# One visit for the experts' down product, a 128-row turn, and a split first weight load in a fused attention and expert kernel

## The chip, the cores and the metric

The kernel runs on one core of a Trainium2 chip. The core has TensorE (matrix products out of SBUF into PSUM), VectorE, ScalarE and GpSimd (element work), and SyncE, whose queue issues most of the transfers between HBM and SBUF; 16 DMA engines move the data. The time is the device's, in microseconds, for one whole execution, and what is compared is the median of several runs.

## The reference, cut to what matters

Two things are computed from one input x of 2048 rows and 1024 columns and mixed row by row with a gate g: a linear attention with 32 heads whose features are softmaxes, and one expert, a gated feed-forward net that sees a single row of x (the one with the largest r) and adds its result to that row alone.

```python
def reference(A_x, A_wqkv, A_w_phi, A_wo, B_x, B_w_r, B_w_gate, B_w_up, B_w_down, gate_w):
    ...
        pq = jnp.einsum("bhsd,hdf->bhsf", q, w_phi)
        pk = jnp.einsum("bhsd,hdf->bhsf", k, w_phi)
        phi_q = jnp.concatenate([_softmax(pq, axis=-1), _softmax(-pq, axis=-1)], axis=-1)
        phi_k = jnp.concatenate([_softmax(pk, axis=-1), _softmax(-pk, axis=-1)], axis=-1)
        kv = jnp.einsum("bhsf,bhsd->bhfd", phi_k, v)
        z  = jnp.einsum("bhsf->bhf", phi_k)
        num = jnp.einsum("bhqf,bhfd->bhqd", phi_q, kv)
        den = jnp.einsum("bhqf,bhf->bhq", phi_q, z)[..., None] + 1e-6
        o = num / den
    ...
        g = _silu(x_sel @ w_gate)
        u = x_sel @ w_up
        y = (g * u) @ w_down
    ...
    x = A_x
    g = _sigmoid((x * gate_w).sum(-1, keepdims=True))
    a = _A_ref(x, A_wqkv, A_w_phi, A_wo)
    b = _B_ref(x, B_w_r, B_w_gate, B_w_up, B_w_down)
    return g * a + (1 - g) * b
```

The expert's hidden width is 3584, so its three weight matrices are 7.3 MB each; all of them are read for the sake of one row.

## The kernel before

The 2048 rows are 16 tiles of 128 (`NT`); x stands transposed in `xT`, with the 1024 columns as 8 blocks of 128 (`KB`). The feature matrix `w_phi` is folded into the key and query weights (`kfold`, `qfold`), so that a feature unit is one product of x with a folded weight: eight 512-column matmuls for a tile and half the heads, 32 units for the keys and 32 for the queries (`NU` = 32).

The program has four stretches in time.

First the value product. `v_first` (from line 611 in the rows) takes row tiles 0 and 1, transposes them on TensorE (line 299), and then goes block by block through the value weights `wv_sb`, which SyncE's queue loads in eight transfers of 256 KB, one for each block (line 282). The columns are cut at `VC` = 0, 256, 640, 1026 into three parts c; block 0 is taken for both tiles with parts 0 and 1 ahead of part 2, blocks 1 to 6 in rounds of six matmuls. Behind the weight loads the same queue issues transposing loads of the further x tiles (line 305), four small loads of `w_phi` and transposing loads of the key and query weights (line 312). Tiles 2 to 15 follow with `k_v` (line 594); the folds of the key weights (line 322) stand after tiles 4, 6, 8 and 9.

Then a loop over steps i. Steps 0 to 31 make the key units (`feats`, line 640) and, five steps later (`LAG`), their sums with the values (`k_kv`, line 671). Steps 32 to 63 make the query units; each unit's features are turned by a transposing DMA on SyncE's queue (line 688, `phT`), and some steps later `q_num` (line 705) multiplies them with the key-value sums, which ScalarE copies out of PSUM at step 36 (`kv_finish`, line 680). The output product (`q_wo`, line 744) follows when a counter of TensorE time, `pe`, says so.

The expert is strewn between these steps. At steps 9, 16 and 23 `ffn_gu` (line 530) makes the gate and up sums: four column strips of 32 run side by side in the array, so the matmuls are marked 128\*32. Their rows are gathered in `gT`, an FP32 tile of 128 partitions that was set to zero at the start and of which 64 rows are filled. At step 29 `ffn_turn` (line 494) turns `gT` into 56 columns of `ffn_ps` by a product with `identf`, with rows 0 to 63 of both. At step 38 (`DN` = 38) `ffn_down(0, 4)` starts the down product, and at step 41 (`DN2` = 3) `ffn_down(4, 7)` ends it: chunk c is four blocks of 128 rows of the down weights, each block is two matmuls of 512 columns (line 548), also on four column strips, so 32 and 24 matmuls. The seven loads of 1 MB each (line 490) are in the code of `ffn_down(0, 4)`; their buffers are those that the gate and up weights leave. `moe_cols`, behind the second visit, copies the sums out of PSUM (line 558), and four small DMAs on SyncE's queue pick the rows (line 560). `moe_sum`, `moe_scale`, `moe_out` and `moe_spread` are placed 4, 6, 7 and 10 steps after `DN + DN2`.

Order: the code above is a list of operations with their dependencies. A planner lays each engine's instructions out from it, earliest possible first, except for what `pin` keeps in place. So a load may stand in a queue long before the step in whose code it is, while TensorE, which always has work ready, runs nearly in the order of the steps.

```python
    DN, DN2 = NU + 6,3
        if i == DN:
            ffn_down(0, 4)
        if i == DN + DN2:
            ffn_down(4, 7)
            moe_cols()
```

Of the kernel before, what the change touches and what calls it, by code (L numbers as in the profile page):

```python
# [20 lines left out]
D = 1024  # L21
# [8 lines left out]
NU = NT * 2  # L30
# [4 lines left out]
VC = [0, 256, 640, 1026]  # L35
# [135 lines left out]
def kernel(  # L171
# [4 lines left out]
    nc = tc.nc  # L176
    x2 = A_x.rearrange("b s d -> (b s) d")
    out2 = out.rearrange("b s d -> (b s) d")
    w_v = A_wqkv.rearrange("(kb p) n -> p kb n", p=P)
# [22 lines left out]
    pin = tc.keep_in_program_order  # L202
# [28 lines left out]
    identf = const.tile([P, 56], F32, name="identf")  # L231
    nc.vector.tensor_copy(out=identf[:], in_=ident[:, 0:56])
    nc.vector.tensor_tensor(out=identf[:, 48:56], in0=identf[:, 48:56], in1=ident[:, 56:64], op=ALU.add)
    gT = const.tile([P, P], F32, name="gT")
# [15 lines left out]
    ffn_ps = small_ps[:, 0:64]  # L250
# [19 lines left out]
    def xload(t, eng):  # L270
        xt_ = shv[1][:, 2 + t, :]
        pin(eng.dma_start(out=xt_, in_=x2[t * P:(t + 1) * P, :]))
        xtiles[t] = xt_

    wv_sb = w16.tile([P, KB, VW], BF, name="wv_sb", tag="w16")
# [3 lines left out]
    for kb in range(KB):  # L279
        if kb == 0:  # L280
            xload(1, nc.sync)
        pin(nc.sync.dma_start(out=wv_sb[:, kb, 0:D], in_=w_v[:, kb, 2 * D:3 * D]))

    def rows_in():
        rows_ps = m2_ps[:, 0:2 * KB]
# [202 lines left out]
    def wd_load(c, where):  # L488
        w = wbuf(where).rearrange("p (b n) -> p b n", b=4)
        nc.sync.dma_start(out=w, in_=wd_v[:, c * 4:(c + 1) * 4, :])  # L490
        return w

    def ffn_turn():
        nc.tensor.matmul(ffn_ps[:, 0:56], lhsT=gT[0:64, :], rhs=identf[0:64, :], start=True, stop=True)

    def ffn_mid():
        sg = const.tile([P, NFB], F32, name="sg")
# [43 lines left out]
    def ffn_down(c0, c1):  # L541
        if c0 == 0:
            moe["wd"] = [wd_load(c, p) for c, p in enumerate("AAADDWV")]
        ws = moe["wd"]
        for blk in range(4 * c0, 4 * c1):
            for n in range(2):
                g = (blk % 2) * 2 + n
                nc.tensor.matmul(small_ps[32 * g:32 * g + 32, :], lhsT=hh32[:, blk, :],  # L548
                                 rhs=ws[blk // 4][:, blk % 4, n * 512:(n + 1) * 512], start=(blk < 2),
                                 stop=(blk >= NFB - 2), tile_position=(0, 32 * g), skip_group_check=True)  # L550

    def moe_cols():
        ym = ring.tile([P, D * 2], F32, name="ym", tag="wch")
        ys = ym[:, 0:512]
        y4 = ym[0:KB, 512:768].rearrange("p (s c) -> p s c", s=2)
        ybc = ym[:, 1280:1792].bitcast(BF)
        moe["ybc"] = ybc
        nc.scalar.copy(out=ys, in_=small_ps[:])
        for g in range(4):
            nc.sync.dma_start(out=y4[4 * (g % 2):4 * (g % 2) + 4, g // 2, :], in_=ys[32 * g:32 * g + 1, :])  # L560
        moe["y4"] = y4
# [238 lines left out]
    QT0, QT1 = (4, 7)  # L800
    GU = (9, 16, 23)
    TU = 29
    DN, DN2 = NU + 6,3
    TF, TNUM, TWO, TKV = 1.73, 0.27, 1.73, 0.27
    L_NUM0, N_1, L_NUM1, L_NUM, L_WO0, L_WO, MOST = 11.0, 6, 15.0, 10.5, 8, 6, 2
    pe = 0.0
# [3 lines left out]
    i = 0  # L810
    while i < 2 * NU or n_next < NU or wos:
# [8 lines left out]
        if i == 28:  # L820
            moe["wo"] = w16.tile([P, KB, D], BF, name="wo_sb", tag="w16")
            nc.gpsimd.tensor_copy(out=moe["wo"][0:1, 0, 0:1], in_=kst[i - 1][0:1, 0, 0, 0:1])
            nc.sync.dma_start(out=moe["wo"][:], in_=A_wo.rearrange("(kb p) n -> p kb n", p=P))
        if i == DN:
            ffn_down(0, 4)
        if i == DN + DN2:
            ffn_down(4, 7)
            moe_cols()
            qp["oo"] = wob.tile([P, 16, 512], BF, name="oo", tag="wo")
            qp["n_oo"] = 0  # L830
            qp["late"] = []
# [27 lines left out]
        if i == TU:  # L859
            ffn_turn()  # L860
            ffn_mid()
# [93 lines left out]
```

## Time and profile before

| what | us |
|---|---|
| median of 3 runs (265.38 to 265.94) | 265.49 |
| the profiled execution, its own time | 264.34 |
| its span, first to last instruction | 262.7 |
| TensorE busy (98% of the span) | 258.3 |
| VectorE, ScalarE, GpSimd busy | 176.2, 128.1, 126.3 |

Rows of the trace come from the one profiled execution. In a timeline each row is a run of like instructions: its start, the time from its first start to its last end, engine, line, tiles, shape and count. A matmul is pipelined: the printed time of one (0.38 us for 512 columns) reaches past the start of the next, so the cost of a matmul on TensorE is read from start to start. The mark 128\*128, 128\*32 or 64\*128 is the part of the array that a matmul takes, rows by columns. PEld rows are the weight loads that go ahead of the matmuls. An idle time in brackets names what ended it; "issue" means nothing that the profile shows.

### The profile page before, as it was taken

The page shows a single profiled execution, that of the slowest core. Times are in us where ns is not written, and L with a number is a line of the kernel's source. Part 1 is how long each engine was busy: PE and PEld are TensorE (multiplying, and loading weights), DVE is VectorE, ACT ScalarE, POOL GpSimd, SP SyncE. Part 2 cuts the span into 40 slices and gives each one's busy share as a digit, 9 for nine tenths or more (in the row PEclk, how much of TensorE's full clock was granted, in tenths as well). Part 3 has the DMA queues.
Part 4 walks back from the last instruction along what each step waited for, and adds up shares of the span by engine and source line. Part 5 has one row for each costly group of instructions (what it writes and reads, how often), then busy time and mean ns, then how long its engine had stood idle before and what let it go on. Part 6 is the DMA issues. An engine that isn't in the chain of part 4 may idle for free.

```text
span 262.7 us, 5700 instructions
## 1 busy us (share of the span) xinstructions
PE 258.3 (98%) x2190; PEld 137.3 (52%) x2190; DVE 176.2 (67%) x309; ACT 128.1 (49%) x264; POOL 126.3 (48%) x86
## 2 busy tenths in 40 slices
PE   8999999999999999999999999999999999999995
PEld 4666666665444554545455455455444544454443
DVE  3111103015599676997888799799898797888873
ACT  3135536356766454654457677447362553535220
POOL 7000000000175998679989887655535545454101
PEclk9999999999999999999999999999999999999999
DMA  6999999949999959989968997997989697879642
GB/s 220 267 138 188 169 177 186 187 94 364 406 349 162 227 145 415 395 300 368 376 201 317 218 153 200 223 203 136 261 179 232 139 225 164 211 144 192 165 126 82
DMA packets 110971, 58.47 MB, mean 223 GB/s; under 512 B 93580, under 2 KB 98780, under 8 KB 110940
## 3 DMA queue, kind: packets, MB, share of 16 engines
q1 hardware_dynamic: 108252, 53.73, 84.3%
q10 hardware_dynamic: 2656, 4.33, 6.2%
q8 instruction: 18, 0.29, 0.5%
q14 instruction: 13, 0.11, 0.1%
q0 software_dynamic: 32, 0.00, 0.0%
HBM read 31.27 MB, written 4.20 MB: 135 GB/s over the span
## 4 chain that ended last, share of the span: by engine, by line
PE 95%; DVE 2%; ACT 1%; issue 0%; ACTq 0%; DVEq 0%
PE pq L640 21%; PE po L744 21%; PE pk L640 20%; PE pv L594 18%; PE kvps L671 3%; PE num L705 3%; PE facc L530 2%; PE pv L611 1%; PE vbank L611 1%; PE small_ps L548 1%; PE small_ps L206 1%; PE vbank L322 1%; DVE wfT L343 1%; DVE xT L301 1%; PE vbank L338 0%
## 5 line engine op out<-in xcount | busy, mean ns | idle before, releaser
L658 POOL TENSOR_TENSOR phi<-e,rq 128x1024 bf16<-128x1024 bf16 x63 | 119.6, 1912 | 65.2 <-DVE rq L654 50.0
L650 DVE TENSOR_REDUCE ssum<-e 128x32 f32<-128x1024 bf16 x64 | 77.4, 1211 | 16.6 <-ACT e L646 16.5
L640 PEld LDWEIGHTS <-xT 128*128 128x128 bf16 x512 | 47.3, 97 | 52.7 <-issue 1.4
L640 PE MATMUL pq<-wqf,xT 128*128 128x512 bf16 x256 | 60.3, 379 | 0.0
L640 PE MATMUL pk<-wkf,xT 128*128 128x512 bf16 x256 | 59.9, 379 | 0.1
L744 PE MATMUL po<-wo_sb,oT 128*128 128x512 bf16 (+2 forms) x264 | 60.0, 372 | 0.0
L594 PE MATMUL pv<-wv_sb,xT 128*128 128x256 bf16 (+2 forms) x336 | 50.2, 307 | 0.0
L594 PEld LDWEIGHTS <-xT 128*128 128x128 bf16 x336 | 31.9, 97 | 16.1 <-issue 0.5
L645 ACT ACTIVATE e<-pq 128x512 bf16<-128x512 f32 x32 | 18.9, 592 | 36.1 <-PE pq L640 35.7
L602 ACT CAST v_all<-pv 128x384 bf16<-128x384 f32 (+1 forms) x45 | 20.1, 450 | 33.5 <-PE pv L594 25.1
L744 PEld LDWEIGHTS <-oT 128*128 128x128 bf16 x264 | 23.9, 98 | 23.3
L645 ACT ACTIVATE e<-pk 128x512 bf16<-128x512 f32 x32 | 19.2, 599 | 27.2 <-PE pk L640 21.8
L748 DVE SCALAR_TENSOR_TENSOR oo<-po,gate,xg 128x512 bf16<-128x512 f32 (+2 forms) x33 | 24.0, 727 | 4.4 <-PE po L744 4.3
L472 POOL COPY wch<-shv 1x1 bf16<-1x1 bf16 x3 | 0.4, 176 | 52.5 <-DMA shv<-in_A_wqkv_dram 52.5
L654 DVE RECIPROCAL rq<-ssum 128x32 f32<-128x32 f32 x64 | 21.8, 342 | 1.3
L326 DVE CAST wkf<-vbank 128x512 bf16<-128x512 f32 x8 | 5.2, 687 | 25.8 <-PE pW L322 25.8
L710 DVE TENSOR_TENSOR o_sb<-num,rden 128x512 bf16<-128x512 f32 x32 | 21.6, 674 | 0.8
L646 ACT ACTIVATE e<-pk 128x512 bf16<-128x512 f32 x32 | 19.0, 594 | 0.0
L646 ACT ACTIVATE e<-pq 128x512 bf16<-128x512 f32 x32 | 18.9, 590 | 0.0
L729 ACT ACTIVATE xg<-xin,omg 128x1024 f32<-128x1024 bf16 x16 | 18.4, 1148 | 0.4
L705 PEld LDWEIGHTS <-phT 128*128 128x128 bf16 x256 | 12.4, 98 | 7.8 <-issue 0.5
L343 DVE CAST wfT<-vbank 128x512 bf16<-128x512 f32 x8 | 5.2, 683 | 16.1 <-PE pW L338 16.1
(134 smaller groups left out, 155.2 us busy)
## 6 DMA issues: line engine op xcount, KB each, us to landing
wch<-in_B_w_down_dram SPq DMA_DIRECT2D x7, 1024.0 KB
wch<-in_B_w_up_dram SPq DMA_DIRECT2D x6, 1024.0 KB
wch<-in_B_w_gate_dram SPq DMA_DIRECT2D x4, 1024.0 KB
xin<-in_A_x_dram ACTq DMA_DIRECT2D x16, 256.0 KB
out_dram<-oo SPq DMA_DIRECT2D x31, 128.0 KB
wch<-in_B_w_gate_dram SPq DMA_DIRECT2D x4, 768.0 KB
wv_sb<-in_A_wqkv_dram SPq DMA_DIRECT2D x8, 256.0 KB
wo_sb<-in_A_wo_dram SPq DMA_DIRECT2D x1, 2048.0 KB
```

The lines of the kernel that those rows point to most:

```text
L594: nc.tensor.matmul(pv[:, 0:hi - lo], lhsT=xT[:, kb, t * P:(t + 1) * P], rhs=wv_sb[:, kb, lo:hi], start=(kb == 0), stop=(kb == KB - 1))
L602: copy(out=v_all[:, t, h0:h1, 0:DH], in_=pv[:, 0:(h1 - h0) * DH].rearrange("p (h d) -> p h d", d=DH))
L640: nc.tensor.matmul(pk[:].rearrange("p (c r) f -> p c r f", r=4) if is_q else pkf, lhsT=xT[:, kb, t * P:(t + 1) * P], rhs=q_heads(wf, kb, h ...
L645: nc.scalar.activation(out=e[:, :, 0, :], in_=pk[:], func=ACTF.Exp)
L646: nc.scalar.activation(out=e[:, :, 1, :], in_=pk[:], func=ACTF.Exp, scale=-1.0)
L650: nc.vector.tensor_reduce(out=ssum[:], in_=e2, axis=AX.X, op=ALU.add)
L654: nc.vector.reciprocal(out=rs, in_=ssum[:])
L658: eng.tensor_tensor(out=phi[:].rearrange("p h s f -> p (h s) f"), in0=e2, in1=_bc(rs, [P, HH * 2, DH]), op=ALU.mult)
L705: nc.tensor.matmul(num[:, pl * 66:pl * 66 + 66], lhsT=phT[:, pl, :], rhs=KV[hf][:, pl, :], start=True, stop=True)
L710: nc.vector.tensor_tensor(out=st["o"][:, hf * HH:(hf + 1) * HH, :].rearrange("p (r h) d -> p r h d", h=2), in0=nv[:, :, :, 0:DH], in1=rden ...
L744: nc.tensor.matmul(po[:, 0:w], lhsT=st["oT"][:, kb, :], rhs=moe["wo"][:, kb, sl], start=(kb == 0), stop=(kb == KB - 1))
L748: nc.vector.scalar_tensor_tensor(out=o_out[:, 0:w], in0=po[:, 0:w], scalar=gate[:, t:t + 1], in1=st["xg"][:, sl], op0=ALU.mult, op1=ALU.add)
```

## The change

Three edits. The down product becomes one visit of 56 matmuls at step 40, `ffn_down(0, 7)`, with its loads, its sums' copies and the steps that hang on `DN + DN2` one step earlier than before (the copy `hh32` stays at step 35). The turn of the gate and up sums uses all 128 rows of `gT` and `identf`, of which rows 64 and up are zero. The load of block 0 of the value weights is issued as two transfers, columns 0 to 255 and 256 to 1023.

```diff
     for kb in range(KB):
         if kb == 0:
             xload(1, nc.sync)
-        pin(nc.sync.dma_start(out=wv_sb[:, kb, 0:D], in_=w_v[:, kb, 2 * D:3 * D]))
+        for lo, hi in ((0, VC[1]), (VC[1], D)) if kb == 0 else ((0, D),):
+            pin(nc.sync.dma_start(out=wv_sb[:, kb, lo:hi], in_=w_v[:, kb, 2 * D + lo:2 * D + hi]))
...
     def ffn_turn():
-        nc.tensor.matmul(ffn_ps[:, 0:56], lhsT=gT[0:64, :], rhs=identf[0:64, :], start=True, stop=True)
+        nc.tensor.matmul(ffn_ps[:, 0:56], lhsT=gT[:], rhs=identf[:], start=True, stop=True)
...
-    DN, DN2 = NU + 6,3
+    DN, DN2 = NU + 6, 2
...
-        if i == DN:
-            ffn_down(0, 4)
         if i == DN + DN2:
-            ffn_down(4, 7)
+            ffn_down(0, 7)
             moe_cols()
```

## Rows read from the trace of the kernel before

**Rows 1.** The page's busy table: engine, busy us, share of the span, instructions.
```profile
PE 258.3 (98%) x2190; PEld 137.3 (52%) x2190; DVE 176.2 (67%) x309; ACT 128.1 (49%) x264; POOL 126.3 (48%) x86
```
**Rows 2.** TensorE's timeline, 135.9 to 138: start, length, engine, line, operation, tiles, count.
```profile
135.97 1.89 PE L640 MATMUL pq<-wqf,xT 128*128 128x512 bf16 x8
137.69 0.42 PE L671 MATMUL kvps<-v_all,phi 128*128 128x66 bf16 x8
```
**Rows 3.** TensorE's timeline at the first down visit, 147.3 to 148.9 and 143 to 160.
```profile
147.12 0.38 PE L640 MATMUL pq<-wqf,xT 128*128 128x512 bf16 x1
...
147.43 1.91 PE L548 MATMUL small_ps<-wch,hh 128*32 128x512 bf16 x32
149.28 1.90 PE L640 MATMUL pq<-wqf,xT 128*128 128x512 bf16 x8
```
**Rows 4.** TensorE's timeline at the second down visit, 143 to 160.
```profile
155.32 1.48 PE L548 MATMUL small_ps<-wch,hh 128*32 128x512 bf16 x24
156.74 1.90 PE L640 MATMUL pq<-wqf,xT 128*128 128x512 bf16 x8
```
**Rows 5.** Line 490, the loads of the down weights: duration min/median/max, first and last start.
```profile
L490 SPq DMA_DIRECT2D wch<-in_B_w_down_dram x7: 367/467/3902, 102.5 to 133.1; - x7
```
**Rows 6.** Timelines of SyncE's queue and of ScalarE ahead of the down product.
```profile
142.85 11.70 SPq L688 DMA_TRANSPOSE phT<-phi  x6
...
146.24 0.38 ACT L680 CAST KV<-kvps 64x264 bf16<-64x264 f32 x1
```
**Rows 7.** SyncE's queue in the first 24 us, and TensorE at 23 us.
```profile
1.78 3.75 SPq L282 DMA_DIRECT2D wv_sb<-in_A_wqkv_dram  x8
...
17.54 1.31 SPq L312 DMA_TRANSPOSE shv<-in_A_wqkv_dram  x1
...
23.12 0.19 PE L322 MATMUL vbank<-BDm,shv 32*128 32x32 bf16 x3
```
**Rows 8.** Timelines of TensorE and of its weight loads at the turn, 131.0 to 132.1.
```profile
131.07 0.38 PE L640 MATMUL pk<-wkf,xT 128*128 128x512 bf16 x1
131.38 0.42 PE L494 MATMUL small_ps<-identf,gT 64*128 64x56 f32 x2
131.74 0.43 PE L671 MATMUL kvps<-v_all,phi 128*128 128x66 bf16 x8
...
131.38 0.29 PEld L494 LDWEIGHTS small_ps<-identf,gT 64*128 64x128 f32 x2 [0.42 <-issue]
```
**Rows 9.** TensorE's timeline at a small full-array product, 108.2 to 109.2.
```profile
108.61 0.17 PE L421 MATMUL small_ps<-hlb,const-bfloat16-1.0 128*128 128x2 bf16 x1
108.64 0.41 PE L671 MATMUL kvps<-v_all,phi 128*128 128x66 bf16 x8
```
**Rows 10.** TensorE's timeline in the first value product, 5 to 12.7.
```profile
4.77 0.58 PE L299 MATMUL pT<-ident,shv 128*128 128x128 bf16 x6
5.18 0.47 PE L611 MATMUL vbank<-wv_sb,xT 128*128 128x256 bf16 x2
...
6.30 0.60 PE L611 MATMUL vbank<-wv_sb,xT 128*128 128x256 bf16 x3
6.75 0.60 PE L611 MATMUL pv<-wv_sb,xT 128*128 128x256 bf16 x3
7.30 0.60 PE L611 MATMUL vbank<-wv_sb,xT 128*128 128x256 bf16 x3
```
**Rows 11.** DMA packets of three stretches, in order 4.5:5.5, 5.5:9.25 and 10.5:11.75.
```profile
DMA packets 135, 0.25 MB, mean 246 GB/s; under 512 B 15, under 2 KB 15, under 8 KB 135
...
DMA packets 781, 1.43 MB, mean 381 GB/s; under 512 B 84, under 2 KB 84, under 8 KB 781
...
DMA packets 1394, 0.35 MB, mean 279 GB/s; under 512 B 1394, under 2 KB 1394, under 8 KB 1394
```
**Rows 12.** TensorE's timeline at a late start in the query steps, 210.8 to 211.7.
```profile
210.53 0.81 PE L640 MATMUL pq<-wqf,xT 128*128 128x512 bf16 x3
211.38 0.42 PE L705 MATMUL num<-KV,phT 128*128 128x66 bf16 x8
```

## The prediction

> **What bounds the kernel now.** I read the page's busy table first: TensorE works through 98% of the span [rows 1]. So a gain has to be time that TensorE loses between matmuls, and a loss has to be a new wait of TensorE; what VectorE, ScalarE, GpSimd and the queues save counts for nothing unless TensorE was waiting for it. Next I read TensorE's timeline, where one thing must be watched: matmuls overlap, so the duration printed is not their cost. The cost is the distance from one start to the next. In a plain stretch eight 512-column matmuls of the query projection start at 135.97 and the next group at 137.69 [rows 2]: 1.72 / 8 = 0.215 us each, and the eight 66-column matmuls behind them are as dense. Against this beat I looked for starts that come late, at the three places of the change. All three show one.
>
> **Part 1, the down product in one visit.** The last query matmul ahead of the first visit starts at 147.12 [rows 3]; at 0.215 us the next would start at 147.335, but the first down matmul starts at 147.43: 0.095 us lost on entry. The visit is 32 matmuls, four at a time on the four column strips, so eight groups; 149.28 - 147.43 = 1.85 us, less 8 x 0.215 = 1.72, leaves 0.13 us lost inside and on leaving. The second visit is six groups: 156.74 - 155.32 = 1.42, less 1.29, again leaves 0.13 [rows 4]. So a visit costs about 0.22 us beside its work, whatever its size, and one visit of 14 groups instead of two saves 0.22 us. The work itself, 14 x 0.215 = 3.0 us, stays.
>
> What moves with it. (a) The seven loads of the down weights now stand in step 40's code and not in step 38's. The queue took them at 102.5 to 133.1 [rows 5], long before step 38 ran at 147.4, because the planner puts a load where its buffer falls free; the last goes out 14 us ahead of its first use. Two steps' later place changes nothing as long as they stay ahead of the key and query transposes, the first of which goes out at 142.85 [rows 6]; if one slid behind those it would still have the 4 us by which the visit starts later. Cost: none, cover 14 us. (b) Two query units and the first two numerator steps come earlier by the first visit, 1.94 us. The first numerator stands behind the query unit that starts at 149.28 [rows 3], so it started at 149.28 + 1.72 = 151.0, and would start at about 149.07. It needs phi's first transpose, issued at 142.85 [rows 6], 6.2 us before; elsewhere a transpose issued at 17.54 feeds a matmul at 23.12, 5.6 us later, without a wait [rows 7]. It also needs the last copy of the key-value sums, which starts at 146.24 and takes 0.38 [rows 6]: 2.4 us of cover. Cost: none. (c) The wide copy of the down sums, the four row copies on SyncE's queue and the steps that follow go out some 2 us sooner; nothing on TensorE waits for them until the last output tiles. (d) The planner lays the order of the instructions anew. Its price is a rival below.
>
> **Part 2, the turn with 128 rows.** The last key matmul ahead of it starts at 131.07; the next start is due at 131.285, and the first turn matmul starts at 131.38 [rows 8]: the same 0.095 us as on entry to the down product. From there to the next stream is 131.74 - 131.38 = 0.36 us, for two matmuls of only 56 columns (the FP32 product is issued as a pair). The weight loads show why: in the plain stretch they lie under the matmul before, here the load starts only at 131.38 after an idle time of 0.42 [rows 8]. So the 64-row form pays for a change of array shape as the 32-column form does. With all 128 rows the shape is that of its neighbours, and both losses, 0.095 and up to 0.13, should go: about 0.20 us. The trace has no FP32 matmul at 128 rows, so bounds: the nearest full-array insert, two columns in BF16, costs 108.64 - 108.61 = 0.03 us [rows 9]; were the two turn matmuls that cheap, the stay of 0.455 us would fall to 0.06, a gain of 0.39. At the other end both FP32 loads (a pair took 0.29 us, rows 8, about 0.18 each) lie open: 0.36 + 0.06 = 0.42, a gain of 0.03; a little below nothing, -0.05, if the wider load is slower still. I take 0.20, nearest to the measured losses of the same kind.
>
> The page TensorE: Matmul & The Clock Gate of the Trainium skill, Part 3, The mechanism, says that a weight load overlaps matmuls in flight only when its row group differs. By that rule a 128-row load could never hide behind a 128-row matmul, and the change would gain nothing on entry. The BF16 loads of rows 2's stretch speak against it, since they leave no gap; no row here shows it for FP32.
>
> **Part 3, block 0 of the value weights in two pieces.** The first value matmul starts at 5.18 [rows 10], directly behind the transposes of x; TensorE is busy up to it, so landing the first 256 columns sooner gains nothing there. The load bound comes after: a round of six matmuls takes 0.88 us, three of them 0.44, but from 6.75 to 7.30 three took 0.55 [rows 10]. The only operand new at 7.30 is block 2. So the stream of blocks is already about 0.11 us late there, and whatever delays blocks 1 and 2 is passed on to TensorE in full; from block 3 on the stream gains on TensorE again (0.262 MB at 381 GB/s is 0.69 us a block [rows 11], against 0.88).
>
> The two pieces make 256 packets of 512 and 1536 bytes out of 128 of 2048. In the stretch of 2 KB packets the queue moved 381 GB/s, in one of 256-byte packets 279 [rows 11]. A block at 279 takes 0.94 us: at most +0.25 us. The lower end is 0, or -0.1 if the late start at 7.30 goes by chance. By packets: 3.75 x 16 / (781 - 84) = 86 ns for one of 2 KB, 1.25 x 16 / 1394 = 14 ns for one of 256 bytes, so a fixed part of some 4 ns; eight more packets on each of the 16 engines is 0.03 us, and one more completion. I take +0.10 us.
>
> The extra issue costs SyncE 3.75 / 8 = 0.47 us [rows 7], and all that stands behind it in that queue (blocks 1 to 7, the x and weight transposes) goes out as much later. The blocks wait for their bandwidth, not for their issue (the last is issued by 1.78 + 3.75 = 5.53; ten blocks of 0.262 MB, two of x and eight of weights, take 6.9 us even at 381 GB/s, so the stream lasts past 6.9), so this is covered; the transpose for 23.12 was issued 5.6 us ahead. If that cover is not there, it is the second rival.
>
> **Sum.** -0.22 - 0.20 + 0.10 = -0.32 us. The profiled execution took 264.34 us, 262.7 of it span: 264.02 after. The median of the runs shown, 265.49, lies 1.15 above it: 265.17, so 265.2. That is 0.12%; a change under 0.2% (0.53 us) is about what a measurement of this kernel can't tell from none.
>
> **Rivals.**
> (A) The 128-row FP32 load isn't hidden; the turn gains 0.03. Sum -0.15: 265.35. For it: no such row. Against: the entry loss is exactly that of a changed shape.
> (B) The extra issue slot reaches TensorE: blocks 1 and 2 come 0.47 later, without slack. -0.42 + 0.47 = +0.05: 265.55. For it: block 2 is late already. Against: each block goes out 0.47 us behind the last and takes 0.69 us to move, so the queue runs ahead of the stream, and further with every block.
> (C) Slower. The stream of blocks has one bad microsecond, 4.5 to 5.5, at 246 GB/s [rows 11]. If the two pieces spread that rate over the stream, a block takes 1.07 us against TensorE's 0.88, and blocks 2 to 7 cost 6 x 0.19 = 1.15, less the 0.11 there now: +1.04 - 0.42 = +0.62, 266.1. It decides once the stream falls below 0.262 / 0.88 = 300 GB/s. Against: the stream recovers to 381 right after.
> Beside (C): DMA: Bandwidth & Descriptors of the Trainium skill, Measured, gives 0.95 us for a transfer of 64 KB and advises transfers of 1 MiB and more; by it the first piece alone would cost 0.78 us more than its share of the stream, and the sum would be near +0.4. Blocks of 0.26 MB at 381 GB/s don't bear that out, as they run into one another.
> (D) The planner's new order puts matmuls ahead of their operands. The trace has such a wait: three matmuls at 210.53 are followed at 211.38, 0.20 later than 3 x 0.215 [rows 12]. Two to four more: 265.6 to 266.0.
> (E) The turn falls to its lower bound and the late start at 7.30 is not made worse: -0.22 - 0.39 - 0.0 to 0.1 = -0.6 to -0.7: 264.8.
>
> **How the numbers follow.** Forecast 0.42, A 0.13, B 0.12, C 0.07, D 0.12, E 0.14. Faster by over 0.2%: E and a little of the forecast's lower end, 0.20. Slower by over 0.2%: C and the worse part of D, 0.12. Within: 0.68. The range: from E's time to the middle of D, 264.75 to 265.95.
>
> **What would show it.** After: one run of 56 down matmuls whose next start is 3.01 + 0.13 us behind its first; a turn marked 128*128 that starts 0.215 us behind the key matmul before it, and a weight load without the idle 0.42; block 1 or 2 late by 0.1 to 0.2 us in all in the start, at 6.3 to 7.5. The prediction is wrong if the first numerators wait, if the turn stays near 0.45 us, if a round of the value product at the start takes over 1.0 us, or if new late starts of 0.2 us stand elsewhere.

## The result and the profile after

| kernel | runs | median us | range us |
|---|---|---|---|
| before, beside the change | 5 | 265.55 | 265.38 to 265.94 |
| the change | 5 | 268.17 | 266.52 to 269.75 |
| before, beside a later set | 23 | 265.31 | 264.58 to 267.50 |
| the change, in that set | 12 | 267.13 | 265.52 to 269.79 |

The ratio was 1.010 (95% interval 1.005 to 1.015), in the larger set 1.005 (1.0015 to 1.0086). By the medians the change is slower by 1.8 to 2.6 us, where -0.3 had been forecast; the ratio of the larger set, which leaves out two executions of the change that lie over 1.5% above its fastest, says 0.4 to 2.3. Single executions of one kernel lie up to 4 us apart, so differences of some tenths are read from the traces below and not from medians.

The profiled execution of the change took 268.17 us, with a span of 266.5 (before: 264.34 and 262.7). TensorE's work is the same; its share fell because the span grew. From the page:

```profile
PE 258.4 (97%) x2190; PEld 137.3 (52%) x2190; DVE 175.6 (66%) x309; ACT 128.4 (48%) x264; POOL 126.2 (47%) x86
```

Five distances cut the span where the change touches it; each is a difference of two times in the traces. A is the end of the first value product (the first matmul of row tile 2); B the turn, from the last key matmul ahead of it to the next stream; C from there to the first output product; D from that to TensorE's last instruction; E from VectorE's last work to the end. Between A and B stand 118.5 to 118.7 us in every kernel, between D and E 0.46.

| profiled execution | A | B | C | D | E |
|---|---|---|---|---|---|
| before | 12.59 | 0.67 | 30.95 | 96.87 | 2.66 |
| the change | 13.17 | 0.38 | 31.51 | 97.93 | 4.53 |
| the change, second execution | 13.07 | 0.38 | 31.51 | 98.19 | 3.41 |
| difference, first and second | +0.58, +0.48 | -0.29 | +0.56 | +1.06, +1.32 | +1.87, +0.75 |

The differences add up to +3.8 and +2.8 us, as the spans do. One of the five is a gain. Each has its lines in the trace of the change.

**A**, TensorE's timeline at the start (of before: [rows 10]): the first value matmul runs, and the second waits for the second piece of block 0.

```profile
5.37 0.27 PE L612 MATMUL vbank<-wv_sb,xT 128*128 128x256 bf16 x1
6.23 0.34 PE L612 MATMUL vbank<-wv_sb,xT 128*128 128x384 bf16 x1 [0.58 <-DMA wv_sb<-in_A_wqkv_dram]
```

**B**, TensorE and its weight loads at the turn, now marked 128\*128 (before: [rows 8]).

```profile
131.93 0.32 PE L495 MATMUL small_ps<-identf,gT 128*128 128x56 f32 x2
132.09 0.42 PE L672 MATMUL kvps<-v_all,phi 128*128 128x66 bf16 x8
...
131.72 0.41 PEld L495 LDWEIGHTS small_ps<-identf,gT 128*128 128x128 f32 x2
```

**C**, TensorE from 147 to 157, and ScalarE ahead of it (before: [rows 3, 4]).

```profile
147.68 0.23 PE L706 MATMUL num<-KV,phT 128*128 128x66 bf16 x2
148.12 1.89 PE L641 MATMUL pq<-wqf,xT 128*128 128x512 bf16 x8 [0.21 <-ACT e L647]
...
151.85 0.40 PE L549 MATMUL small_ps<-wch,hh 128*32 128x512 bf16 x3
152.18 0.43 PE L706 MATMUL num<-KV,phT 128*128 128x66 bf16 x8
152.54 3.19 PE L549 MATMUL small_ps<-wch,hh 128*32 128x512 bf16 x53
155.66 1.69 PE L641 MATMUL pq<-wqf,xT 128*128 128x512 bf16 x7
```
```profile
143.60 0.94 ACT L820 COPY hh<-hh 128x896 bf16<-128x896 bf16 x1
...
145.41 1.16 ACT L681 CAST KV<-kvps 64x264 bf16<-64x264 f32 x3
...
146.58 0.38 ACT L681 CAST KV<-kvps 64x264 bf16<-64x264 f32 x1
146.98 0.60 ACT L646 ACTIVATE e<-pq 128x512 bf16<-128x512 f32 x1
147.47 0.59 ACT L647 ACTIVATE e<-pq 128x512 bf16<-128x512 f32 x1
```

ScalarE has the wide copy `hh32` (0.94 us) and four copies of the key-value sums on top of its exponentials, and is behind. The query unit of 148.12 needs the PSUM buffer that the exponential of 147.47 frees at 148.06: 0.37 us later than the beat. (The planner has put two of the first numerator's eight matmuls ahead of that unit, at 147.68, and six behind it.) Before, the first down visit stood at this place (147.43 to 149.28), and ScalarE caught up under it. And the "one visit" is two again: a numerator stands behind its first three matmuls.

**D**, TensorE at numerator 14, SyncE's queue ahead of it, and the link of the critical chain that ends there.

```profile
188.12 1.89 PE L641 MATMUL pq<-wqf,xT 128*128 128x512 bf16 x8
190.89 0.43 PE L706 MATMUL num<-KV,phT 128*128 128x66 bf16 x8 [0.88 <-DMA phT<-phi]
```
```profile
180.00 0.39 SPq L584 DMA_DIRECT2D ym<-ydr  x1
180.49 1.24 SPq L721 DMA_TRANSPOSE oT<-o_sb  x1
181.83 2.40 SPq L689 DMA_TRANSPOSE phT<-phi  x1
```
```profile
181.83 9.02 DMA phT<-phi
```

The features' transpose takes 9.02 us from issue to landing and makes TensorE 1.05 us late. Ahead of it stand an output transpose and the spread of the expert's row to 128 partitions (line 584).

**E**, SyncE's last checks, from the landing of the last store to the drain: line, operation, count, durations in ns, first and last start.

```profile
L949 SPq EVENT_SEMAPHORE  x8: 27/28/28, 265.1 to 265.6; - x8
```

In before, the same stretch has one check:

```profile
L950 SPq EVENT_SEMAPHORE  x1: 28/28/28, 261.7 to 261.7; - x1
```

### The profile page after: what moved, and what is told of

Read it like the earlier page. It is cut to its first block, busy times and chain, and to the rows that moved or that the text cites. A ratio compares the mean times of both kernels' runs of the same rounds, so it can differ in the third digit from the quotient of the medians.

```text
span 266.5 us, 5701 instructions
## 1 busy us (share of the span) xinstructions
PE 258.4 (97%) x2190; PEld 137.3 (52%) x2190; DVE 175.6 (66%) x309; ACT 128.4 (48%) x264; POOL 126.2 (47%) x86
## 4 chain that ended last, share of the span: by engine, by line
PE 85%; DMA 5%; DVE 4%; ACT 3%; issue 1%; SPq 0%; ACTq 0%; DVEq 0%
PE pk L641 19%; PE pv L595 18%; PE po L745 18%; PE pq L641 16%; DMA phT<-phi 3%; PE kvps L672 3%; PE num L706 3%; PE facc L531 2%; DMA wv_sb<-in_A_wqkv_dram 1%; PE vbank L612 1%; DVE ssum L651 1%; PE pv L612 1%; PE small_ps L549 1%; DVE o_sb L711 1%; ACT e L647 1%; ACT e L646 1%
## 5 line engine op out<-in xcount | busy, mean ns | idle before, releaser
L672 PEld LDWEIGHTS <-phi 128*128 128x128 bf16 x256 | 11.9, 98 | 7.5 <-POOL phi L659 0.8
```

## Experiments

Every kernel is the kernel before with the edit shown, except where another base is named. Where a ratio is given there are 12 timed runs against 23 to 35 of before.

**1. The turn alone.**

```diff
-        nc.tensor.matmul(ffn_ps[:, 0:56], lhsT=gT[0:64, :], rhs=identf[0:64, :], start=True, stop=True)
+        nc.tensor.matmul(ffn_ps[:, 0:56], lhsT=gT[:], rhs=identf[:], start=True, stop=True)
```

> Only the turn of the gate and up sums uses all 128 rows. The order of every engine's instructions is that of before. Theory T (the 64-row shape costs an entry and an exit, and the FP32 load of 128 rows hides under the matmul before it): the stay from the last key matmul to the next stream falls from 0.67 us between starts to about 0.47, and the time by 0.20 us, to about 265.3. Rival (the load isn't hidden, and the fall seen in the changed kernel came from elsewhere): within 0.05 us.

Measured: ratio 0.9997 (0.9972 to 1.0022), median 265.11 against 265.24; span 262.4. B is 0.38 in place of 0.67, and all else stays as in before, in the same order on every engine:

```profile
131.07 0.41 PEld L494 LDWEIGHTS small_ps<-identf,gT 128*128 128x128 f32 x2
```

The FP32 load now starts together with the last key matmul; in before it started 0.31 later [rows 8]. The turn is a gain of 0.29 us, and too small for the medians.

**2. The cut of block 0 alone**, and a second profile of it.

```diff
+        for lo, hi in ((0, VC[1]), (VC[1], D)) if kb == 0 else ((0, D),):
```

> Only block 0 of the value weights is loaded in two pieces; all else as before. Theory S (the second piece, 1536 bytes a row, falls into the slow microsecond of the load stream at 4.5 to 5.5 and is wanted at 5.3, where before that microsecond fell on block 1, wanted at 6.3): TensorE waits 0.5 to 0.9 us for it at 5.3 to 6.3, the time goes up by 0.5 to 0.8 us, to about 266.2, and no other wait appears later. Rival (the late piece in the changed kernel's profile was chance, a slow transfer of one execution): within 0.2 us of before.

> The cut of block 0 alone, a second profiled execution of the same kernel. If the late second piece and the late last store belong to the cut: TensorE again waits 0.7 to 1.3 us between its first two value products, the first product ends after 13.1 us, and the last stretch again takes 4.1 to 4.5 us. If they were chance: the last stretch 2.6 to 2.8 us, and the first product ends between 12.6 and 13.4 us as with the uncut block.

Measured: ratio 1.0015 (0.9987 to 1.0042), median 265.99 against 265.24. A was 13.88 and 13.08, E was 4.14 and 3.07. The wait between the first two value matmuls is in both (1.28 and 0.63 us); of the second profile:

```profile
5.35 0.42 PE L612 MATMUL vbank<-wv_sb,xT 128*128 128x256 bf16 x1
6.08 0.39 PE L612 MATMUL vbank<-wv_sb,xT 128*128 128x384 bf16 x1 [0.32 <-DMA wv_sb<-in_A_wqkv_dram]
```

The timed runs don't tell this kernel from before. In the profiles two things had to be told apart: what the cut does at the start, and what the additional transfer does at the end.

**3. Block 7 cut in place of block 0**, twice.

```diff
+        for lo, hi in ((0, VC[1]), (VC[1], D)) if kb == 7 else ((0, D),):
```

> The same cut into 256 and 768 columns, but of value weight block 7, which is needed last; block 0 is loaded whole. It adds the one transfer without touching the block that TensorE waits for first. Theory (the cut costs because the block needed first lands in two pieces, each among other transfers): first value products as in before (end of the first product 12.6 to 13.4 us with the scatter that kernels with an uncut block 0 showed), median within 0.3 of before. Rival (an extra transfer as such costs, by shifting the rings and semaphores of all later ones): the last store lands 1.5 to 1.9 us later as in both profiles with the cut, the last stretch from VectorE's last work to the end takes 4.1 to 4.5 us and not 2.6 to 2.8, median 266 or more.

> Block 7 cut, a second profiled execution. All five executions of kernels with the one more transfer had a last stretch (VectorE's last work to the end) of 3.07 to 4.53 us, eight of nine without it 2.57 to 2.82, the ninth 3.74. If the transfer as such makes the end later, it is over 3.0 us once more; if the five were chance, 2.6 to 2.8 us is as likely. The first value products run as with the uncut block.

Measured: ratio 1.0016 (0.9984 to 1.0048), median 265.49 against 264.97. E was 3.10 and 3.21, neither 2.6 to 2.8 nor over 4. A was 12.59 and 13.53, and the second shows that an uncut block 0 is late as well; TensorE waits for the whole of it:

```profile
6.49 0.43 PE L612 MATMUL vbank<-wv_sb,xT 128*128 128x256 bf16 x2 [1.21 <-DMA wv_sb<-in_A_wqkv_dram]
```

SyncE's checks behind the last store's landing, of the second profile:

```profile
L951 SPq EVENT_SEMAPHORE  x8: 27/28/28, 262.8 to 263.2; - x8
```

SyncE's and ScalarE's transfers report on a ring of eight semaphores, taken in turn, and at the end SyncE checks the eight in order. In all eleven profiles of kernels without the extra transfer the last store reports on the eighth, and the program ends 0.96 to 0.97 us after that. With the transfer every later one moves on by a place, the last store reports on the first, seven checks are still to be made behind it, and the end comes 1.39 to 1.40 us after: 0.43 us in each of six profiles.

**4. Block 0 cut, blocks 6 and 7 in one transfer.** The count is as before.

```diff
+        for lo, hi in ((0, VC[1]), (VC[1], D)) if kb == 0 else ((0, D),) if kb < 6 else ():
...
+    pin(nc.sync.dma_start(out=wv_sb[:, 6:8, 0:D], in_=w_v[:, 6:8, 2 * D:3 * D]))
```

> Block 0 cut as in the change, and blocks 6 and 7, which are needed last, loaded by one transfer, so that the queue's transfers are again as many as before. In six profiles with the one more transfer the last store reported on the ring's first semaphore, SP still had seven checks to make behind it, and the program ended 1.39 us after that report; in ten without it the report came on the last semaphore and the end 0.97 us after. If that count is the cause, the report is on the last semaphore again, no check is left, the end comes 0.97 us after it, although block 0 is cut; what is left of the cut's cost is at the start, median 0 to 0.4 us over before. If the cut itself is the cause: 1.39 us and seven checks again.

Measured: one check, and the end 0.97 us after the landing.

```profile
L952 SPq EVENT_SEMAPHORE  x1: 28/28/28, 263.8 to 263.8; - x1
```

With block 0 cut and the count restored, the seven checks are gone: the count is the cause of the 0.43 us. The kernel was no better for it: ratio 1.0032 (1.0007 to 1.0057), median 266.29 against 265.08, above the 0 to 0.4 us expected. In its profile A is 13.26, and the last store landed 3.01 us after VectorE's last work, against 12.59 and 1.70 in before; these two make up 2.0 of the 2.1 us by which its span is longer. Why the store was late isn't shown, and the joined load of blocks 6 and 7 is an edit of its own.

**5. The down product in one visit at step 40**, with the steps behind it one earlier as in the change; a second profile of it; and the same with those steps where before has them (the last line, with 6, 7 and 10 likewise).

```diff
-    DN, DN2 = NU + 6,3
+    DN, DN2 = NU + 6, 2
...
-        if i == DN:
-            ffn_down(0, 4)
...
-            ffn_down(4, 7)
+            ffn_down(0, 7)
...
-        if i == DN + DN2 + 4:
+        if i == DN + 7:
```

> Only the down product is merged, at step 40, with the steps that hang on it one earlier; loads and turn as before. Theory M (three losses: the first query unit after the key-value copies waits 0.4 us for ScalarE, which the first visit used to cover; a numerator is planned into the visit, so that it stays two visits; the spread of the expert's row slows the queue ahead of a features' transpose, which comes 1 us late): 0.6 us lost by 158 us of the span and about 1 us more near 190, time about 267.1, and single runs wide apart, over 1 us, because the last wait hangs on transfers. Rival (the losses after 140 us of the changed kernel come from its late start, through the split): the visit gains 0.2 us, 265.3, and runs within 0.6 us of each other.

> The single visit at step 40 with the four steps one step earlier, a second profiled execution. If the wait at numerator 14 belongs to this kernel, it is there again with 0.8 to 1.2 us near 191 us, and the wait of 0.37 us for the exponentials near 148 us and the cut visit with it; the four kernels with only one of the two edits had none. If it was an accident: no wait there, while the other two stay.

> The down product merged at step 40, but the sum, the scale, the store and the spread of the expert's row stay at their old steps 45, 47, 48 and 51. Theory M (the place of the spread makes the 1 us wait near 190): that wait is gone, the 0.6 us by 158 us stay, time about 266.1, and the runs lie closer together than with the steps moved. Rival (the wait comes from the planner's order of the transposes on SyncE's queue, whatever the spread does): the wait near 190 stays, 267.

Measured: 1.0025 (1.0005 to 1.0046) with the earlier steps, 1.0027 (1.0000 to 1.0053) without, medians 266.34 and 265.48 against 265.24. C is 31.52 in all three. D is 97.92 and 97.84 with the earlier steps, 96.86 without. That microsecond is read from the profiles: the two ratios don't tell the kernels apart. The second profile has the wait again:

```profile
190.84 0.43 PE L705 MATMUL num<-KV,phT 128*128 128x66 bf16 x8 [0.80 <-DMA phT<-phi]
```

**6. The earlier steps alone**, with two visits (and likewise 6, 7 and 10).

```diff
-        if i == DN + DN2 + 4:
+        if i == DN + DN2 + 3:
```

> Two visits as before; alone the four steps behind them (sum, scale, write and spread of the expert row) stand one step earlier, as the change has them. Theory (the wait of 1.05 us near 190 us comes from the earlier steps, whose transfers and an output transpose now stand ahead of a late feature transpose on SP's queue): the wait of about 1.0 us at numerator 14 is there although the visits are not joined, everything ahead of 185 us stays as before, median about 266.2, 0.9 to 1.0 over before. Rival (the wait comes from the joined visit and its shifted copies): no wait near 190 us, median within 0.2 of before.

A miss: ratio 0.9997 (0.9963 to 1.0030), and numerator 14 starts on the beat although SyncE's queue has the new order, the output transpose ahead of the features'.

```profile
178.21 0.38 SPq L583 DMA_DIRECT2D ym<-ydr  x1
178.68 1.24 SPq L720 DMA_TRANSPOSE oT<-o_sb  x1
180.02 1.85 SPq L688 DMA_TRANSPOSE phT<-phi  x1
```
```profile
188.58 0.81 PE L640 MATMUL pq<-wqf,xT 128*128 128x512 bf16 x3
189.22 0.42 PE L705 MATMUL num<-KV,phT 128*128 128x66 bf16 x8
```

So it takes both edits. The transpose of numerator 14, by the semaphores of the traces:

| kernels | issue to landing us | issue to need us |
|---|---|---|
| both edits (4 profiles) | 8.3 to 9.1 | 7.1 to 7.8 without the wait |
| not both, landing over 5 us (10 profiles) | 5.0 to 7.2 | 8.5 to 9.2 |
| not both, landing under 5 us (3 profiles) | 4.1 to 4.3 | 7.0 to 7.9 |

The transposes just before it (numerator 13) take 3.1 to 3.7 us in all of these. In the thirteen profiles a slow landing came with an early issue and a late issue with a quick landing; with both edits a slow landing meets a late issue.

The spread alone doesn't set the landing. In twelve of the thirteen it is issued 0.44 us ahead of the transpose, and the landing still takes 4.1 to 7.2 us. What differs among the twelve is when ScalarE's queue issues its load of a tile of x (line 698 in before; 256 KB, 128 packets of 2 KB):

| nearest loads of x, by their issue against the transpose's | profiles | issue to landing us |
|---|---|---|
| 0.71 to 1.61 us ahead | 3 | 4.1 to 4.3 |
| from 0.04 ahead to 0.14 behind | 3 | 5.0 to 5.4 |
| 0.22 to 0.58 behind | 6 | 5.8 to 7.2 |
| both edits: one 0.70 to 1.35 ahead, a second 0.43 to 1.08 behind | 4 | 8.3 to 9.1 |

Experiment 6 has another order in the queue, with the loads 0.49 and 2.31 us behind, and took 6.7. The loads ahead of and behind the transpose, in the trace of experiment 1 (transpose issued at 180.75) and of the change (181.83):

```profile
179.84 0.33 ACTq L698 DMA_DIRECT2D xin<-in_A_x_dram  x1
183.93 0.33 ACTq L698 DMA_DIRECT2D xin<-in_A_x_dram  x1
```
```profile
181.13 0.33 ACTq L699 DMA_DIRECT2D xin<-in_A_x_dram  x1
182.91 0.33 ACTq L699 DMA_DIRECT2D xin<-in_A_x_dram  x1
```

No run moves a load of x alone, so this is an order seen in the traces and not a cause shown. It fits the other transposes: numerator 18's, with loads of x and no spread near, took 3.7 to 6.6 us, numerator 25's 3.0 to 3.1 in all eighteen profiles.

**7. The spread on ScalarE's queue**, in the first kernel of experiment 5 (one visit at step 40, the steps behind it one earlier).

```diff
     def moe_spread():
-        nc.sync.dma_start(out=moe["ybc"], in_=...)
+        nc.scalar.dma_start(out=moe["ybc"], in_=...)
```

> The single visit at step 40 with the four steps one step earlier, where alone the spread of the expert row goes to ScalarE's queue; the order on SP is otherwise that of the kernel with the wait, the output transpose ahead of the feature transpose. If the feature transpose is late because it stands behind the spread's packets on the same queue, it lands within 7 us of its issue (8.8 to 9.1 us in the four executions with the wait, 5.9 to 7.2 in those without) and numerator 14 does not wait. If it is late because of the output transpose put ahead of it, or because the engines that move the data are slow whatever the queue, the wait of about 1 us stays.

Measured: 272.1 us in a single run, and the question was only half answered, as everything behind 178 us had moved. ScalarE took the spread in program order and stood until the row had been written:

```profile
178.75 0.36 ACTq L583 DMA_DIRECT2D ym<-ydr  x1
179.21 0.60 ACT L645 ACTIVATE e<-pq 128x512 bf16<-128x512 f32 x1 [4.30 <-PE pq L640]
...
182.53 0.60 PE L705 MATMUL num<-KV,phT 128*128 128x66 bf16 x8 [3.71 <-DVE o_sb L710]
```

VectorE waited for that exponential, and TensorE for VectorE. But the features' transpose that ran beside the spread's packets, now that of numerator 13, took 6.90 us, where it takes 3.1 to 3.7 elsewhere, although the spread was in another queue. So a transpose need not stand behind the spread to be slow. Which transfer slows it stays open: ScalarE issued a load of x at 179.32, 0.64 us behind this transpose (178.68), and this run can't tell it from the spread. The Trainium skill, DMA: Bandwidth & Descriptors, Issuing engines are not separate DMA queues, says that what the engines issue runs on the same 16 DMA engines. The 6.90 us, with the spread and the load of x both in another queue, agrees.

**8. The visit of 56 pinned at step 40; the visit at step 38.** The first is experiment 5 with the later steps of before and this:

```diff
-                nc.tensor.matmul(small_ps[32 * g:32 * g + 32, :], lhsT=hh32[:, blk, :], ...)
+                pin(nc.tensor.matmul(small_ps[32 * g:32 * g + 32, :], lhsT=hh32[:, blk, :], ...))
```

The second moves nothing else:

```diff
         if i == DN:
-            ffn_down(0, 4)
+            ffn_down(0, 7)
         if i == DN + DN2:
-            ffn_down(4, 7)
```

> The visit of 56 at step 40 with all later steps as before, and its matmuls held in the order written, so that no numerator comes between them. If the 0.56 us that the stretch from the turn to the first output product gained has two causes, the wait for the exponentials (0.37) and the numerator that cuts the visit (0.2 for the second entry and partial group), the second is gone and the first stays: stretch about 31.3 us (30.95 before, 31.52 with the cut visit). If the cut visit cost nothing: 31.5 again. If the wait hung on the same numerator: 30.7.

> One visit of 56 down products as in the change, but at step 38, where the first of the two visits stood, and all later steps as before. Theory (the single visit at step 40 lost time because the first visit had covered ScalarE's backlog near 147 us, and because a numerator cut the visit in two): nothing waits for the exponentials near 148 us, the 56 products stand in one piece, and the stretch from the last key product ahead of the turn to the first output product goes from 30.95 to about 30.73 us; no wait near 190 us; median about 265.0, 0.2 under before. Rival (joining the visits is worth nothing or costs by itself): the stretch stays at 30.95 us or grows toward the 31.5 of the visit at step 40, median 265.3 to 265.9.

Measured: step 40 pinned, 265.25 in a single run; step 38, ratio 1.0011 (0.9979 to 1.0043). What a visit costs, from the beat that follows the matmul ahead of it to the start of the next stream:

| kernel | matmuls | us |
|---|---|---|
| before | 32 and 24 | 1.94 + 1.50 = 3.44 |
| change; visit at step 40 (3 profiles) | 3 and 53 | 0.42 + 3.22 = 3.64 |
| pinned at step 40; at step 38 | 56 | 3.23 |

C was 31.10 pinned: 30.95 + 0.37 for the wait for ScalarE, which stayed, - 0.21. (D was 97.14, with 0.48 in place of 0.20 at the numerator near 212.) At step 38 that wait is gone:

```profile
147.92 3.21 PE L548 MATMUL small_ps<-wch,hh 128*32 128x512 bf16 x56
151.06 1.90 PE L640 MATMUL pq<-wqf,xT 128*128 128x512 bf16 x8
...
212.10 0.42 PE L705 MATMUL num<-KV,phT 128*128 128x66 bf16 x8 [0.31 <-DVE o_sb L710]
```

The gain of 0.21 us is there as forecast, and a new order of the later units takes it back: numerators wait for VectorE, 0.18 us near 164 and 0.47 instead of 0.20 near 212, so C + D is 128.05 against 127.82.

**9. What gained, together:** the edits of experiment 1 and of step 38 in experiment 8; twice.

> The turn of 128 rows and the single visit at step 38, with all later steps as before and block 0 uncut: what of the change has shown a gain. If both gains add, the turn's stay is 0.377 us in place of 0.666 and the visit saves 0.22: 0.5 us less in front of the output products. The visit at step 38 alone gave 0.45 of that back in two waits of numerators for a normalised output (0.18 at 164 us, 0.27 at 211 us); if they are there again, the kernel is 0.1 under before in its profile, about 265.0, and within 0.2 per cent. If they were accidents of that execution, it is 0.5 under before, 264.6.

> The turn of 128 rows and the single visit at step 38 once more, for a second set of timed runs and a second profile. Its first profile had a stretch of 0.29 and of 0.21 us less, two waits that gave 0.45 back, and an end of 3.74 us where kernels with the same transfers had 2.57 to 2.82. If that end was chance, it is 2.6 to 2.8 us now, the span 262.6 or less plus what the first block's landing gives, and the median again 0.1 to 0.6 us under before. If it belongs to this kernel: over 3.5 us again and no gain.

Measured: ratios 0.9979 (0.9951 to 1.0008) and 1.0018 (0.9988 to 1.0048), medians 265.11 and 265.24 against 265.31 and 265.08. B, C and D were 0.38, 30.47 and 97.58 in both, 0.06 us less than before in all, and the last store landed late in both (E 3.74 and 3.00, with one check). No kernel tried here was measurably faster than before.

## Why the prediction was wrong, step by step

The two gains were forecast rightly in kind. What failed are four terms put at nothing or too low: what the query unit needs (part 1 (b)), what the earlier steps' transfers do to a transpose (part 1 (c), the largest), where the start of the value product comes from (part 3), and what one more transfer moves at the end (no part).

**Part 1, the price of a visit: right.** 0.22 forecast, 0.21 measured in the two kernels whose visit stays whole.

**Part 1 (b), "Cost: none": wrong, 0.37 us.** The step asked what the numerators need and found it early enough, rightly. It did not ask what the query unit needs that now comes 1.94 us sooner: the PSUM buffer that ScalarE frees. The work that made ScalarE late stood in the rows the step used [rows 6]. The first visit was a cover for it.

**Part 1 (d), rival D: right in kind.** The planner did put a numerator where it costs, into the visit: +0.20 instead of -0.21, 0.41 us beside the forecast. With 0.37 that is C: -0.21 + 0.41 + 0.37 = +0.57, measured 0.56.

**Part 1 (c), "nothing on TensorE waits for them": wrong, 1.05 and 1.31 us, the largest term shown to belong to the change.** True of the results, false of the transfers: numerator 14 waits for its transpose in the four profiles with both edits, and in none of the thirteen with one of them or neither. The joined visit and the earlier steps, each harmless here alone (experiments 5 and 6), together used up a slack of 2.4 us: before, numerator 14's transpose landed at 186.32 and was needed at 188.72. With both it is issued 1.3 to 1.9 us nearer to its need and takes 8.3 us and more, with the spread and two loads of x issued close around it. Which of these slows it stays open.

**Part 2: the mechanism right, the size 0.29 for 0.20.** The entry loss of 0.095 is gone: the turn starts 0.215 us behind the key matmul. The stay of 0.36 fell to 0.16, by 0.20 and not 0.13 at most. The rule of rival A (the Trainium skill, TensorE: Matmul & The Clock Gate, Part 3, The mechanism) fails here: a 128-row FP32 load went under a 128-row matmul, at 131.07. The same section also lets a load go ahead into the background weight buffer, which the prediction left out and this trace agrees with.

**Part 3: wrong in its base.** That the first value matmul starts directly behind the transposes, "so landing the first 256 columns sooner gains nothing there", was read from one execution in which block 0 landed at 4.98, earlier than in any other of 13 with it uncut (5.18 to 6.45). In 11 of those 12 the first value matmul starts 0.04 to 0.05 us behind that landing. So the landing does set the start, and the cut does what it is for: the first matmul at 5.37 (median of five) against 5.82. But the second, 0.11 us of work later, needs the second piece, and it comes at 6.08 against 5.93; A is 13.17 against 12.93. Cost 0.24 us where 0.10 was taken, at the upper bound; it is a difference of medians of five and thirteen profiles with a scatter of 0.9 us between executions, which the bounds did not hold, so its size is only roughly known. Rivals B and C are not what happened: behind the late second piece the change's profile has no wait for a further block.

**What no part had: the extra transfer's place in the ring, 0.43 us.** Part 3 counted the transfer's packets and its issue, and looked at what stands behind it in the queue for the next 20 us. What it shifted was 260 us later.

**The sum.** +0.24 - 0.29 + 0.56 + 1.05 to 1.31 + 0.43 = +2.0 to +2.25; measured +1.8 and +2.6 by the medians. (From the parts known by then, +1.8, 266.9 us, had been expected of the larger set; its median was 267.13.) The two profiled executions lost more, 3.8 and 2.8 us: in them the last store landed 3.13 and 2.01 us after VectorE's work, before 1.70. Whether that belongs to the change is open. It took 1.6 to 1.9 us in eleven of the thirteen profiles with block 0 uncut, 2.04 and 2.78 in the two of experiment 9; in the five with block 0 cut it took 1.67, 2.01, 2.74, 3.01 and 3.13. No run shows how a cut at the start could reach the last store, and five profiles are few.

## What to carry to other kernels

Work that is moved away from between two stages may also have been the time in which another engine caught up: list the buffers that the next work needs and who frees them, not only its operands. A slack read from one execution is one draw: where a load decides the start, look at several executions of anything that begins the same way, and where a transfer shares the DMA engines, look at what every queue issues around it. Count transfers: one more moves all later ones by a place, in the order of a queue and in the ring on which they report.

## What the runs showed of the hardware

- A transposing DMA of 128 x 8 x 128 took 3.0 to 3.1 us from issue to landing for numerator 25, in all eighteen profiles, 3.7 to 6.6 for numerator 18, beside loads of x from another queue, and 4.1 to 9.1 for numerator 14, beside such loads and a row spread to 128 partitions.
- The end of this program costs 0.06 us for each semaphore that is checked behind the last landing: 8 checks in place of one, 0.43 us.
- In experiment 7 TensorE stood still from about 178.8 to 182.5. Within that time its granted clock fell from 2.4 GHz to half, 1.2, stayed there while TensorE was busy again, and was back at 2.4 from 188.5 on. Per stretch: length, then busy time of PE, PEld, DVE, ACT and POOL, granted clock, DMA share, GB/s.

```profile
176.00:179.00 3.00, 2.83 (x20) 1.33 (x19) 0.14 (x1) 0.00 (x0) 0.00 (x0) 1.00 0.87 188
179.00:182.50 3.50, 0.00 (x0) 0.00 (x0) 2.17 (x5) 1.52 (x4) 0.43 (x1) 0.88 0.83 158
182.50:187.00 4.50, 4.47 (x25) 2.16 (x25) 3.54 (x7) 3.14 (x8) 1.71 (x2) 0.50 1.18 244
187.00:188.50 1.50, 1.50 (x5) 0.45 (x4) 1.16 (x3) 0.83 (x1) 1.50 (x1) 0.50 0.70 245
188.50:192.00 3.50, 3.50 (x25) 1.73 (x24) 2.15 (x4) 1.09 (x2) 0.18 (x1) 1.00 1.01 186
```

Twelve 512-column matmuls between 182.5 and 188.5 took 0.21 us more each, start to start: 2.5 us on top of the wait.
